# Top-k attention with two feed-forward layers on one core: the first batch's last 64 tokens worked on behind the second batch's first 256, their scores kept in DRAM

## The chip, the cores and the metric

The kernel runs on one core of one Trainium2 chip. The metric is the device time of one execution in microseconds (us). The engines are named as in the profile: PE is the matrix engine (PEld its weight loads), DVE the vector engine, ACT the scalar engine, POOL the general engine, SP the engine that issues nearly all DMAs.

## The reference, cut to what matters

```python
# attention: batch 4, 8 heads, 576 tokens, head dimension 64
scores = (1 / sqrt(64)) * q @ k.T
kth = np.partition(scores, -32, axis=-1)[..., -32]      # 32nd largest of each row
scores = np.where(scores >= kth, scores, -1e9)
attn = softmax(scores) ; x = attn @ v                    # x: 2304 tokens x 512
# two layers, each 512 -> 2048 -> 512, fp32 in and out
h = np.maximum(x @ w_in, 0) ; x = (h * h) @ w_out
h = x @ w_in2 ; out = np.maximum(0.01 * h, h) @ w_out2
```

## The kernel before, in words

**Units, tiles and pairs.** The list `UNITS` cuts the 4 x 576 tokens into nine units (batch, first token, tokens), and its order is the order of the work. Within a unit the kernel takes four head pairs one after the other. A unit of 256 tokens gives four tiles of 128 rows for each head pair, one of 320 tokens gives five, one of 64 tokens gives one (64 rows of each of the two heads). There are 144 tiles in all. Two tiles make a pair; 72 pairs follow each other.

**What is done to a tile.** PE makes its scores (L276, two halves of 288 columns) and ACT copies them to a buffer `s` (L277). DVE finds the 32 largest of each row: four MAX8 (L828) with three MATCH_REPLACE8 (L830) between them. POOL takes a difference of two of the values found (`nb`, L288), ACT turns the scores into weights (L294, L298), and PE transposes them (L312, L325).

**Native and split units.** Units with a number below `NATIVE` multiply weights and values in plain fp32 on PE (L396), and normalise afterwards with a row that PE transposes too (L346). Later units are split: the weights are normalised on POOL (L307), and weights and values are cut into a high and a low part (ACT and DVE for the weights, L317, L318, L334 and L335; ACT and POOL for the values, L113, L115 and L230), so that PE can multiply nine times for each head in the faster fp32r form (L407), with ACT and DVE joining the halves (L412, L413). The buffers of split units exist only when the last native unit is done (`open_late`). Split values are kept in DRAM for the next unit of the same batch (L233, L211).

**Scores kept in DRAM.** Batches 2 and 3 (`EARLY`) have their scores made long before they are used, as filling work in slots 2 to 245. They go through five `stage` buffers to DRAM (L280) and come back 24 slots before their turn (`load_s`, L284). Batches 0 and 1 have their scores made 30 slots ahead, straight into `s`. Keys of a batch are loaded and split once for each head pair (L201, L115, L238), through one raw buffer; the keys of batch 1 take the buffers of batch 0 when the last scores of batch 0 are made.

**Feed-forward blocks.** The tokens, in the order of the units, go into blocks of 512, 256, 384, 512, 256 and 384 tokens (`BLOCKS`). When all tokens of a block are there, its two layers are put into the instruction stream between the attention work: each layer is 16 steps, numbered here 0 to 31 for block 0, 32 to 63 for block 1, 64 to 95 for block 2, 96 to 127 for block 3. A step is 12 matmuls into `h` (L574), an activation on ACT with POOL and in part DVE (L584 to L600), and 8 to 12 matmuls into `acc` (L617 for layer 1, L619 for layer 2). Between the layers ACT and DVE store `xh` and `xl` (L630, L631). During block 0 the weights also come from their raw form: two ACT copies, two DVE operations, one ACT copy and one POOL difference for each of 64 weight tiles (L508, L509, L513, L514, L518, L520).

**What sets the order.** Every piece of attention work has a slot (16 slots to a pair; `z = 16 * p`). The feed-forward work of a block is spread by a rate over the slots until the next block is ready. A scheduler then lays out each engine's fixed instruction order. Tokens of a unit that do not fit into a block are put aside in `spill` (L430) and put into the next one by `unspill` (L447).

Of the kernel before, what the change touches and what calls it, by code (L numbers as in the profile page):

```python
# [24 lines left out]


UNITS = [
    (0, 0, 256), (0, 256, 256), (0, 512, 64), (1, 0, 256), (1, 256, 320),
    (2, 0, 256), (3, 0, 256), (2, 256, 320), (3, 256, 320),
]  # L30

# [6 lines left out]
SPILL = 128  # L38


NATIVE = 3

EARLY = (2, 3)
FILL = (2, 245)
# [12 lines left out]
DLEAD = 30  # L57
LEAD = 24
# [13 lines left out]
def topk_attention_moe_moe2_kernel(  # L72
# [28 lines left out]
    def bank():  # L101
        return psum.tile([P, 512], F, tag="att", name="att", bufs=3)
# [15 lines left out]
    units = []  # L118
# [4 lines left out]
    uhs = []  # L123
    tiles = []
    for u in units:
        for hp in range(NHP):
            n = u["n"]
            uh = dict(u=u, hp=hp, n=n, b=u["b"], first=(u["t0"] == 0), ti=len(tiles), idx=len(uhs),
                      c0=P * (hp % 2) if n == 64 else 0)
            offs = (W - 64 - n, 64)  # L130
            for t in range(2 * n // P):
                lo, hi = t * P, t * P + P
                parts = []
                if lo < n:
                    parts.append((0, offs[0] + lo))
                if hi > n:
                    parts.append((1, offs[1] + lo - n))
                tiles.append(dict(uh=uh, parts=parts, col=uh["c0"] + lo, i=len(tiles)))
            uh["last"] = len(tiles) - 1
            uh["lastA"] = uh["ti"] + (n - 1) // P  # L140
            uhs.append(uh)
    NPAIRS = len(tiles) // 2

    def direct(uh):
        return uh["b"] not in EARLY

    for i, uh in enumerate([uh for uh in uhs if direct(uh)]):
        uh["di"] = i

    def split(uh):  # L150
        return uh["u"]["i"] >= NATIVE

# [5 lines left out]
    for i in range(4):  # L158
        x = const if i < 2 else ahead
# [28 lines left out]
    def at(slot, fn, *a):  # L188
        events.setdefault(slot, []).append((fn, a))


    KT = {}
# [65 lines left out]
    def scores(t, half):  # L258
        uh = t["uh"]
        d = uh["qs"]  # L260
        kt = KT[uh["b"], uh["hp"]]
        if half == 0:
            if direct(uh):
                t["s"] = sbufs[t["i"] % NS]
            else:
                t["s"] = ahead.tile([P, S], F, tag="stage", name="stage", bufs=NST)
        ks = slice(half * HALF, (half + 1) * HALF)
        mm = [(x[:, h, c:c + P], kt[:, h, ks]) for h, c in t["parts"] for x in d]
        if not direct(uh):
            ps = stage_psum.tile([P, 512], F, tag="sp", name="sp", bufs=SPB)  # L270
        elif uh["b"] == 0:
            ps = stage_psum.tile([P, 512], F, tag="sd", name="sd", bufs=SDB)
        else:
            ps = bank()
        for i, (l, r) in enumerate(mm):
            PE.matmul(ps[:, 0:HALF], lhsT=l, rhs=r, start=i == 0, stop=i == len(mm) - 1)  # L276
        ACT.activation(t["s"][:, ks], ps[:, 0:HALF], AF.Copy, scale=0.125)  # L277
        if half == 1 and not direct(uh):
            t["sd"] = dram.tile([P, S], F, tag=f"sd{t['i']}", name=f"sd{t['i']}")
            SP.dma_start(t["sd"], t["s"])  # L280

# [361 lines left out]
    used = {}  # L643
    opened = 16 * (max(uh["last"] for uh in uhs if not split(uh)) // 2) + 35

    def score_slot(ti):
        return 16 * (ti // 2) - DLEAD + 5 * (ti % 2)

    def after(z, *keys):
        return max([z] + [used[k] + 1 for k in keys if k in used])  # L650

    order = []
    for uh in uhs:
        b, hp, i = uh["b"], uh["hp"], uh.get("di")
        z = score_slot(uh["ti"])
        if uh["first"] and direct(uh):
            st = {"i": i}
            st["n"] = len(order)
            order.append(b)
            z0 = after(z - 62, ("kraw", st["n"] - KRB), *[("KT", x, hp) for x in range(b)])  # L660
            at(z0, load_k, b, hp, st)
            for h in range(2):
                at(z0 + 12 * h + 11, split_k, b, hp, st, h)
            used["kraw", st["n"]] = z0 + 23
            assert z0 + 24 <= z
        if (b, hp) not in vdone or split(uh) and VTB < NHP:
            assert not uh["u"]["i"] < NATIVE <= units[max(x["i"] for x in units if x["b"] == b)]["i"]
            vdone.add((b, hp))
            zv = z + DLEAD + 4
            if split(uh):  # L670
                zv = max(zv, opened)
            at(zv, load_v, uh)
            if split(uh):
                at(zv + 6, split_v, uh, 0)
                at(zv + 9, split_v, uh, 1)
        if not direct(uh):
            continue
        uh["qs"] = qsets[i % 2]
        z0 = after(z - 70, ("qraw", i - 2))
        z1 = max(after(z - 20, ("q", i - 2)), z0 + 6)  # L680
        assert z1 + 4 <= z
        at(z0, load_q, uh)
        at(z1, split_q, uh, 0)
        at(z1 + 4, split_q, uh, 1)
        used["qraw", i] = z1 + 4
        used["q", i] = used["KT", b, hp] = score_slot(uh["last"]) + 2

    later_uhs = {}
    for uh in uhs:
# [44 lines left out]
    for p in range(NPAIRS):  # L734
        pr = dict(t=tiles[2 * p:2 * p + 2], p=p)
        pairs.append(pr)
        z = 16 * p
        for i, t in enumerate(pr["t"]):
            if direct(t["uh"]):
                at(z - DLEAD + 5 * i, scores, t, 0)  # L740
                at(z - DLEAD + 2 + 5 * i, scores, t, 1)
            else:
                at(z - LEAD + i, load_s, t)
            if i == 0:
                at(z + 14, shifts, pr)
            at(z + 14 + i, drop, pr, i)
            at(z + 16 + i, expo_sum, pr, i)
            if split(t["uh"]):
                at(z + 20 + i, norm, pr, i)
            at(max(z + 20 + 3 * i, z + 21 + i), pt_main, t)  # L750
        at(z + 18, recip, pr)
        at(z + 26, pt_left, pr)
# [9 lines left out]
    for uh in uhs:  # L762
        if split(uh):
            za, z = 16 * (uh["lastA"] // 2) + 30, 16 * (uh["last"] // 2) + 30
# [7 lines left out]
        for hs in ((0,), (1,)) if apart else ((0, 1),):  # L772
            z = 16 * (uh["lastA"] // 2 if hs == (0,) else uh["last"] // 2) + 30
# [4 lines left out]
        z += nq  # L778
        if uh["u"]["i"] == NATIVE - 1 and uh["hp"] == NHP - 1:
            at(z, open_late)  # L780
# [31 lines left out]
    last = max(events)  # L812
    while slot <= last:
        p, i = divmod(slot, 16)
        if slot >= 0 and p < NPAIRS:
# [7 lines left out]
            x = i % 2  # L823
            t = pr["t"][x]
# [79 lines left out]
```

## Time and profile before

| | |
|---|---|
| median of 3 runs | 1203.64 us (1200.65 to 1205.4) |
| profiled execution | 1204.04 us, of which the trace's span is 1202.3 us |
| busy in the span | PE 1133.4 us (94%), DVE 945.0 (79%), ACT 798.8 (66%), POOL 679.4 (57%) |
| the chain that ended last | PE 56%, DVE 4%, ACT 1%, DMA 1% of the span |
| DMA | 323.25 MB, mean 269 GB/s |

The busy shares are means over stages with different limits. DVE's work ends with the top-k at 957 us; after that it has little to do, while PE has work to the end. So the table says what each engine does, not which one a stage waits for; that is read stage by stage.

### The profile page before, as it was taken

The page shows a single profiled execution, that of the slowest core. Times are in us where ns is not written, and L with a number is a line of the kernel's source. Part 1 is how long each engine was busy: PE and PEld are TensorE (multiplying, and loading weights), DVE is VectorE, ACT ScalarE, POOL GpSimd, SP SyncE. Part 2 cuts the span into 40 slices and gives each one's busy share as a digit, 9 for nine tenths or more (in the row PEclk, how much of TensorE's full clock was granted, in tenths as well). Part 3 has the DMA queues.
Part 4 walks back from the last instruction along what each step waited for, and adds up shares of the span by engine and source line. Part 5 has one row for each costly group of instructions (what it writes and reads, how often), then busy time and mean ns, then how long its engine had stood idle before and what let it go on. Part 6 is the DMA issues. An engine that isn't in the chain of part 4 may idle for free.

```text
span 1202.3 us, 20196 instructions
## 1 busy us (share of the span) xinstructions
PE 1133.4 (94%) x6388; PEld 993.1 (83%) x6388; DVE 945.0 (79%) x1944; ACT 798.8 (66%) x1819; POOL 679.4 (57%) x922
## 2 busy tenths in 40 slices
PE   5999967998899999999999999999999999999998
PEld 4777845886677889988998998888788899999997
DVE  7999999768988899999999999999999920110122
ACT  6999978678999986766665666555675653334322
POOL 7967565677889876456665665545456554004200
PEclk9899978898999999999999999999999999999999
DMA  9868556679889888889988888777676689879974
GB/s 302 288 208 264 204 197 210 219 244 347 312 285 339 297 289 289 291 279 398 332 284 294 266 282 289 221 228 225 198 223 225 191 270 374 253 247 351 353 250 137
DMA packets 110522, 323.25 MB, mean 269 GB/s; under 512 B 17488, under 2 KB 25680, under 8 KB 110416
## 3 DMA queue, kind: packets, MB, share of 16 engines
q1 hardware_dynamic: 107776, 317.24, 78.3%
q10 hardware_dynamic: 2640, 4.72, 1.1%
q8 instruction: 52, 0.85, 0.3%
q14 instruction: 54, 0.44, 0.1%
HBM read 254.54 MB, written 67.37 MB: 268 GB/s over the span
## 4 chain that ended last, share of the span: by engine, by line
PE 56%; DVE 4%; ACT 1%; DMA 1%; issue 0%; POOL 0%; SPq 0%; ACTq 0%
PE h L574 24%; PE acc L617 12%; PE acc L619 12%; PE att L407 3%; PE att L312 3%; DVE m L828 2%; DVE w L830 1%; PE att L325 1%; DVE PTs L318 1%; DMA vraw<-in_v_dram 0%; PE att L276 0%; DVE xl L631 0%; ACT y L634 0%; DMA wi<-wd 0%; ACT e L298 0%
## 5 line engine op out<-in xcount | busy, mean ns | idle before, releaser
L574 PE MATMUL h<-xh,wi 128*128 128x512 f32 (+2 forms) x1280 | 349.2, 345 | 14.4 <-ACT gb L596 4.9
L828 DVE MAX8 m<-w 128x8 f32<-128x576 f32 x432 | 312.9, 747 | 1.4
L574 PEld LDWEIGHTS h<-xh,wi 128*128 128x128 f32 x1280 | 227.5, 191 | 41.7 <-ACT gb L596 6.6
L830 DVE MATCH_REPLACE8 w<-m,w 128x576 f32<-128x576 f32 x288 | 213.2, 742 | 0.7
L574 PE MATMUL h<-xl,wi 128*128 128x512 f32 (+2 forms) x640 | 207.3, 342 | 2.3 <-DVE xl L631 1.3
L600 POOL TENSOR_TENSOR gl<-ga,gh 128x512 fp32r<-128x512 f32 (+2 forms) x160 | 163.3, 1021 | 44.6 <-ACT gh L599 40.6
L617 PE MATMUL acc<-gh,wo 128*128 128x512 f32 (+2 forms) x768 | 155.9, 341 | 0.0
L619 PE MATMUL acc<-wo,gh 128*128 128x512 f32 x576 | 152.4, 399 | 1.5 <-ACT gh L599 1.5
L597 POOL TENSOR_TENSOR ga<-ga,gb 128x512 f32<-128x512 f32 (+2 forms) x80 | 81.6, 1020 | 107.9 <-ACT gb L596 106.9
L294 ACT ACTIVATE e<-s,m 128x576 f32<-128x576 f32 x144 | 112.5, 782 | 39.2 <-DVE m L828 32.1
L617 PEld LDWEIGHTS acc<-gh,wo 128*128 128x128 f32 x768 | 126.2, 189 | 10.9 <-ACT gh L585 0.4
L574 PEld LDWEIGHTS h<-xl,wi 128*128 128x128 f32 x640 | 121.2, 191 | 14.8 <-DVE xl L631 3.7
L619 PEld LDWEIGHTS acc<-wo,gh 128*128 128x128 f32 x576 | 103.8, 188 | 21.6 <-ACT gh L599 2.6
L586 POOL TENSOR_TENSOR ga<-ga 128x512 f32<-128x512 f32 (+2 forms) x80 | 66.4, 830 | 84.7 <-ACT gh L585 76.5
L298 ACT ACTIVATE e<-e,nb 128x576 f32<-128x576 f32 x144 | 110.8, 774 | 4.7 <-POOL nb L288 4.4
L828 DVE MAX8 m<-s 128x8 f32<-128x576 f32 x144 | 103.8, 747 | 8.3 <-ACT s L277 5.1
L830 DVE MATCH_REPLACE8 w<-m,s 128x576 f32<-128x576 f32 x144 | 106.9, 743 | 0.4
L312 PE MATMUL att<-ident,e 128*128 128x128 f32 x576 | 88.5, 281 | 18.3 <-ACT e L298 13.9
L584 ACT ACTIVATE ga<-h 128x512 f32<-128x512 f32 (+2 forms) x80 | 39.2, 490 | 85.5 <-PE h L574 77.1
L307 POOL TENSOR_SCALAR e<-e,rc 128x576 f32<-128x576 f32 x108 | 80.0, 753 | 28.2 <-DVE rc L303 26.2
L312 PEld LDWEIGHTS att<-ident,e 128*128 128x128 f32 x576 | 70.2, 144 | 29.9 <-ACT e L298 18.2
L599 ACT ACTIVATE gh<-ga 128x384 fp32r<-128x384 f32 (+2 forms) x112 | 58.4, 522 | 44.7 <-POOL ga L597 34.8
(94 smaller groups left out, 2153.0 us busy)
## 6 DMA issues: line engine op xcount, KB each, us to landing
wi<-wd SPq DMA_DIRECT2D x160, 512.0 KB, 5.0
wo<-wd SPq DMA_DIRECT2D x160, 512.0 KB, 5.1
wraw<-in_w_dram SPq DMA_DIRECT2D x64, 512.0 KB, 5.8
sd<-stage SPq DMA_DIRECT2D x72, 288.0 KB, 3.5
s<-sd SPq DMA_DIRECT2D x72, 288.0 KB, 4.5
wd<-wi SPq DMA_DIRECT2D x32, 512.0 KB, 5.3
wd<-wo SPq DMA_DIRECT2D x32, 512.0 KB, 6.2
kraw<-in_k_dram SPq DMA_DIRECT2D x16, 576.0 KB, 4.5
```

The lines of the kernel that those rows point to most:

```text
L294: ACT.activation(t["e"], t["s"], AF.Prelu, bias=pr["m8"][:, i, 31:32], scale=-1.0, alpha=1.0 / FAR)
L298: ACT.activation(e, e, AF.Exp, bias=pr["nb"][:, i:i + 1], scale=-FAR, accum_out=pr["sum"][:, i:i + 1])
L307: POOL.tensor_scalar(e, e, pr["rc"][:, i:i + 1], 1.0, op0=OP.mult, op1=OP.mult)
L312: PE.transpose(ps[:, j * P:(j + 1) * P], t["e"][:, j * P:(j + 1) * P], ident)
L574: PE.matmul(h[:, 0:n], lhsT=wi[:, w, c * P:(c + 1) * P], rhs=x[c][y][:, 0:n], start=cnt == 0, stop=cnt == 3 * NK - 1)
L586: POOL.tensor_tensor(a[:, 0:n], a[:, 0:n], a[:, 0:n], op=OP.mult)
L597: POOL.tensor_tensor(a[:, 0:n], a[:, 0:n], b[:, 0:n], op=OP.subtract)
L600: (DVE if j >= GLD else POOL).tensor_tensor(gl[:, 0:n], a[:, 0:n], gh.bitcast(F)[:, 0:n], op=OP.subtract)
L617: PE.matmul(acc[c][:, 0:n], lhsT=wo[:, w, cs], rhs=g[:, 0:n], start=first, stop=last)
L619: PE.matmul(acc[c], lhsT=g[:, cs], rhs=wo[:, w, :], start=first, stop=last)
L828: cur["dve"] = DVE.max(out=m8[:, x, 8 * r:8 * r + 8], in_=t["s"] if r == 0 else t["w"])
L830: cur["dve"] = DVE.match_replace(out=t["w"], in_to_replace=m8[:, x, 8 * r:8 * r + 8], in_values=t["s"] if r == 0 else t["w"], imm_value=NEG)
```

## The change

Three things change together. The unit (batch 0, tokens 512 to 575) moves behind the unit (batch 1, tokens 0 to 255). It is no longer native but split (`NATIVE` is 2). Its scores are still made while batch 0's keys are there, right behind those of the unit before it, but now go to DRAM and come back 24 slots before their turn (`KEPT`).

```diff
 UNITS = [
-    (0, 0, 256), (0, 256, 256), (0, 512, 64), (1, 0, 256), (1, 256, 320),
+    (0, 0, 256), (0, 256, 256), (1, 0, 256), (0, 512, 64), (1, 256, 320),
...
-NATIVE = 3
+NATIVE = 2
+
+KEPT = 3
...
+    def kept(uh):
+        return uh["u"]["i"] == KEPT
+
+    def score_slot(ti):
+        return 16 * (ti // 2) - DLEAD + 5 * (ti % 2)
+
+    for uh in uhs:
+        uh["zs"] = score_slot(uh["ti"])
+        if kept(uh):
+            ahead_of = [x for x in uhs if x["b"] == uh["b"] and x["hp"] == uh["hp"] and x["i0"] < uh["i0"]][-1]
+            uh["zs"] = score_slot(ahead_of["last"]) + 5
+    in_time = sorted([uh for uh in uhs if direct(uh)], key=lambda uh: uh["zs"])
...
-            if direct(uh):
+            if direct(uh) and not kept(uh):
                 t["s"] = sbufs[t["i"] % NS]
             else:
                 t["s"] = ahead.tile([P, S], F, tag="stage", name="stage", bufs=NST)
...
-        if half == 1 and not direct(uh):
+        if half == 1 and (kept(uh) or not direct(uh)):
             t["sd"] = dram.tile([P, S], F, tag=f"sd{t['i']}", name=f"sd{t['i']}")
             SP.dma_start(t["sd"], t["s"])
...
-        used["q", i] = used["KT", b, hp] = score_slot(uh["last"]) + 2
+        used["q", i] = used["KT", b, hp] = (z if kept(uh) else score_slot(uh["last"])) + 2
...
-            if direct(t["uh"]):
+            if kept(t["uh"]):
+                at(t["uh"]["zs"], scores, t, 0)
+                at(t["uh"]["zs"] + 2, scores, t, 1)
+            if kept(t["uh"]) or not direct(t["uh"]):
+                at(z - LEAD + i, load_s, t)
+            else:
                 at(z - DLEAD + 5 * i, scores, t, 0)
                 at(z - DLEAD + 2 + 5 * i, scores, t, 1)
-            else:
-                at(z - LEAD + i, load_s, t)
```

Block 1 (256 tokens) is now exactly the unit (batch 1, 0 to 255), so nothing is spilled into block 2; block 0 has eight pairs of attention work beside it until block 1 is complete, where it had ten, and block 1 has twelve, where it had ten.

Line numbers below are each kernel's own: L115 is L117 after the change, L238 is L252, L288 is L302, L407 is L421, L520 is L534, L574 is L588, L617 is L631.

On POOL, where block 0 begins, before (`KT` and `kraw` are keys, `wi` and `wo` weights, `xl_650` the low part of block 0's input):

```order
L115 TENSOR_SCALAR KT<-kraw 128x576 x2
L238 TENSOR_TENSOR KT<-kraw,KT 64x576
L520 TENSOR_TENSOR wi<-wc,wi 128x512
L238 TENSOR_TENSOR KT<-kraw,KT 64x576
L520 TENSOR_TENSOR wo<-wc,wo 128x512
L288 TENSOR_TENSOR nb<-m_2297 128x2
L302 TENSOR_SCALAR sum<-sum 128x2
```

The same place after the change:

```order
L445 TENSOR_TENSOR xl_650<-xn,xh_649 128x256
L269 TENSOR_TENSOR q_78<-qraw,q_77 128x256
L534 TENSOR_TENSOR wi<-wc,wi 128x512
L534 TENSOR_TENSOR wo<-wc,wo 128x512
L302 TENSOR_TENSOR nb<-m_2373 128x2
L316 TENSOR_SCALAR sum<-sum 128x2
```

The key split of the fourth head pair no longer stands between the first weight differences and ahead of `nb`; it stands further up, ahead of other `nb` rows.

On PE, in step 3 of block 0, before (`PT` and `VN` are the native weights and values):

```order
L574 MATMUL h<-xh_649,wi 128x512 x4
L346 MATMUL att<-ident,rc 128x128 x2
L617 MATMUL acc<-gh,wo 128x512 x8
L396 MATMUL att<-PT,VN 128x64 x20
L617 MATMUL acc<-gl,wo 128x512 x4
```

The unit's 72 split matmuls after the change, in steps 33 and 34 of block 1 (36 of them; the other 36 stand in steps 37 and 38):

```order
L588 MATMUL h<-xh_3272,wi 128x256
L588 MATMUL h<-xl_3273,wi 128x256
L588 MATMUL h<-xh_3272,wi 128x256 x4
L421 MATMUL att<-PTs,VT 128x64 x17
L633 MATMUL acc<-wo,gl 128x512 x4
...
L588 MATMUL h<-xh_3272,wi 128x256 x4
L421 MATMUL att<-PTs,VT 128x64 x19
L631 MATMUL acc<-gh,wo 128x256 x8
```

Forty native matmuls (20 in step 3, 20 in step 7) are gone from block 0, and 72 split ones have come into block 1. On DVE the order moves as a whole: ahead of the last weight conversion of block 0 stand the first MAX8 of 56 tiles before and of 53 after; ahead of block 1's `xl` rows (its middle) 71 and 65; ahead of block 2's 96 and 92; ahead of block 3's 128 and 128.

## Rows read from the trace of the kernel before

**Rows 1.** Stretches of the span: busy us of each engine, clock, DMA.

```profile
core 0: us, PE busy (x) PEld busy (x) DVE busy (x) ACT busy (x) POOL busy (x), PEclk, DMA share, GB/s
...
200.00:329.00 129.00, 120.64 (x572) 98.58 (x573) 105.58 (x205) 106.32 (x223) 96.11 (x103) 0.94 0.80 276
329.00:426.00 97.00, 93.11 (x450) 76.20 (x450) 85.25 (x158) 91.83 (x188) 82.73 (x81) 0.99 0.88 302
426.00:510.00 84.00, 83.21 (x631) 79.17 (x629) 82.34 (x172) 62.05 (x151) 50.42 (x84) 1.00 0.87 294
510.00:658.00 148.00, 143.65 (x914) 136.31 (x913) 146.25 (x308) 93.04 (x216) 92.66 (x140) 1.00 0.92 319
658.00:745.00 87.00, 84.80 (x472) 76.34 (x471) 86.22 (x184) 56.32 (x125) 53.65 (x73) 0.98 0.84 274
```

**Rows 2.** Timeline of ACT and PE where block 3 begins.

```profile
744.78 0.42 ACT L428 ACTIVATE xh<-xf 128x256 fp32r<-128x256 f32 x1 [0.52 <-DVE w L830]
...
745.25 0.50 PE L574 MATMUL h<-xh,wi 128*128 128x512 f32 x1 [0.21 <-ACT xh L428]
```

**Rows 3.** Timeline of DVE: start us, us, what, count.

```profile
505.73 0.74 DVE L830 MATCH_REPLACE8 w<-m,s 128x576 f32<-128x576 f32 x1
...
509.50 1.07 DVE L631 TENSOR_TENSOR xl<-acc,xh 128x256 fp32r<-128x256 f32 x3
...
705.12 1.40 DVE L828 MAX8 m<-s 128x8 f32<-128x576 f32 x2
```

**Rows 4.** Timeline of POOL, ACT and PE where block 0 begins.

```profile
175.30 1.31 POOL L115 TENSOR_SCALAR KT<-kraw 128x576 fp32r<-128x576 f32 x2 [3.14 <-DMA kraw<-in_k_dram]
...
179.51 1.41 POOL L238 TENSOR_TENSOR KT<-kraw,KT 64x576 fp32r<-64x576 f32 x1
...
182.22 0.20 POOL L288 TENSOR_TENSOR nb<-m 128x2 f32<-128x2 f32 x1
...
182.86 0.76 ACT L298 ACTIVATE e<-e,nb 128x576 f32<-128x576 f32 x1
...
183.76 0.48 PE L312 MATMUL att<-ident,e 128*128 128x128 f32 x1 [9.18 <-ACT e L298]
```

**Rows 5.** Timeline of PE: the native 64-token matmuls and what follows them.

```profile
217.28 6.40 PE L396 MATMUL att<-PT,VN 128*128 128x64 f32 x40
...
225.48 0.63 PE L574 MATMUL h<-xh,wi 128*128 128x512 f32 x1
225.91 0.63 PE L574 MATMUL h<-xl,wi 128*128 128x512 f32 x1
...
250.09 1.00 PE L396 MATMUL att<-PT,VN 128*128 128x64 f32 x8
...
251.23 4.34 PE L396 MATMUL att<-PT,VN 64*128 64x64 f32 x32
```

**Rows 6.** Short stretches, columns as in rows 1.

```profile
221.00:228.00 7.00, 7.00 (x23) 5.84 (x23) 5.82 (x14) 2.90 (x7) 3.39 (x6) 0.51 0.80 273
...
281.00:288.00 7.00, 6.66 (x21) 5.49 (x22) 4.73 (x10) 4.75 (x10) 6.71 (x8) 0.65 1.01 359
```

**Rows 7.** Groups by form: line, engine, what, count, busy us, mean ns.

```profile
L294 ACT ACTIVATE e<-s,m 128x576 f32<-128x576 f32 x144 | 112.5, 782 | 39.2 <-DVE m L828 32.1 <-PE att L325 6.6 <-issue 0.3
...
L318 DVE TENSOR_TENSOR PTs<-att,PTs 128x512 fp32r<-128x512 f32 x108 | 72.9, 678 | 3.8 <-ACT PTs L317 2.9
...
L413 DVE TENSOR_TENSOR xf<-att,tmp 64x256 f32<-64x256 f32 x24 | 10.0, 416 | 0.7 <-ACT tmp L412 0.3
```

**Rows 8.** Timeline of PE in block 1.

```profile
472.74 0.28 PE L574 MATMUL h<-xh,wi 128*128 128x256 f32 x1
472.86 0.28 PE L574 MATMUL h<-xl,wi 128*128 128x256 f32 x1
```

**Rows 9.** Waits of DVE, 140 to 460 us: total, times, longest us.

```profile
DVE wc L513 <- ACT att L509: 24.8, 19, 4.5
```

**Rows 10.** DMA issues of the page: count, KB, us to landing.

```profile
s<-sd SPq DMA_DIRECT2D x72, 288.0 KB, 4.5
```

More of the change, by code (lines that the diff above doesn't have):

```diff
@@ L127, in topk_attention_moe_moe2_kernel @@
             n = u["n"]
-            uh = dict(u=u, hp=hp, n=n, b=u["b"], first=(u["t0"] == 0), ti=len(tiles), idx=len(uhs),
+            uh = dict(u=u, hp=hp, n=n, b=u["b"], first=(u["t0"] == 0), i0=u["i"], ti=len(tiles), idx=len(uhs),
                       c0=P * (hp % 2) if n == 64 else 0)
@@ L145, in direct @@
         return uh["b"] not in EARLY
-    for i, uh in enumerate([uh for uh in uhs if direct(uh)]):
+    def kept(uh):
[8 more added lines that the diff above has]
+    in_time = sorted([uh for uh in uhs if direct(uh)], key=lambda uh: uh["zs"])
+    for i, uh in enumerate(in_time):
         uh["di"] = i
@@ L644, in topk_attention_moe_moe2_kernel @@
     opened = 16 * (max(uh["last"] for uh in uhs if not split(uh)) // 2) + 35
-    def score_slot(ti):
-        return 16 * (ti // 2) - DLEAD + 5 * (ti % 2)
     def after(z, *keys):
@@ L652, in topk_attention_moe_moe2_kernel @@
     order = []
-    for uh in uhs:
+    for uh in in_time + [uh for uh in uhs if not direct(uh)]:
         b, hp, i = uh["b"], uh["hp"], uh.get("di")
-        z = score_slot(uh["ti"])
+        z = uh["zs"]
         if uh["first"] and direct(uh):
@@ L666, in topk_attention_moe_moe2_kernel @@
         if (b, hp) not in vdone or split(uh) and VTB < NHP:
-            assert not uh["u"]["i"] < NATIVE <= units[max(x["i"] for x in units if x["b"] == b)]["i"]
             vdone.add((b, hp))
-            zv = z + DLEAD + 4
+            zv = score_slot(uh["ti"]) + DLEAD + 4
             if split(uh):
```

## The prediction

> **What bounds the kernel now.** I read the stretches first, then the timelines where one gives way to the next. Block 0 runs from 200 to 426 us, and there DVE is busy 105.6 of 129 us and 85.3 of 97: it idles 35 us in 226 [rows 1]. PE (120.6 of 129) bounds the first part and ACT (91.8 of 97) the second, because the weights are converted there too; one wait of DVE is named, 24.8 us for ACT's copies of raw weights [rows 9]. From 426 us to 745 us DVE is the full engine: 82.3 of 84, 146.3 of 148, 86.2 of 87 us, and PE stands at 83.2, 143.7 and 84.8 beside it [rows 1]. So block 0 costs DVE idle time, and blocks 1 and 2 are paid for in DVE work, with PE just behind. Block 3 then starts when its last tokens are there: ACT stores the last `xh` at 744.78 us, and the first matmul of block 3 waits 0.21 us for it at 745.25 [rows 2]. From there to the span's end at 1202.3 are 457 us, and PE has work in nearly all of it. The end is therefore set by when DVE has done the tiles of block 3 (the last of them, tile 104, gets its first MAX8 at 705.8, the second of the two that start at 705.12 [rows 3]), plus a tail that the change leaves alone. The work of DVE up to there is nearly the same before and after, so the question is how much DVE idles on the way.
>
> **Block 0's start.** At 175.30 POOL waits 3.14 us for keys, then spends 1.31, 1.40 (a second row of its form, at 176.69) and 1.41 us on their split, and `nb` stands behind that, at 182.22; ACT's exponentials wait for `nb` (182.86) and PE's transposes for them, 9.18 us idle [rows 4]. The order after the change has these keys further up, since the keys of batch 0 are free earlier. 3.14 + 1.31 + 1.40 + 1.41 is 7.3 us; I take 7 off the start of block 0, at least 0 (if `nb` waits for the two weight differences instead), at most 7.3. DVE is busy through most of that stall, so it gains some 2 us itself.
>
> **Native matmuls out of block 0.** The trace has two records for each fp32 matmul. The first group takes 6.40 us, the second 1.00 and 4.34 us [rows 5]: 11.7 us. Behind the first group the granted clock is 0.51 from 221 to 228 us [rows 6], and a matmul of 512 columns starts every 0.43 us (225.48 and 225.91) [rows 5]. About 4.4 us of feed-forward matmuls, to 228.0, run at 1.2 GHz, and would take half: 2.2 us more. Against it, 9 more split matmuls of 256 columns fall into these 16 steps, 9 x 0.12 [rows 8] = 1.1 us. PE bounds there, so 11.7 + 2.2 - 1.1 = 12.8; I take 12, since step and conversion chain do not shrink for sure. Bounds: 6 and 13.
>
> **Two pairs fewer beside block 0.** The order has 22 tiles transposed in the 32 steps before, 20 after, and 26 fewer score matmuls (13 fewer ACT copies). On ACT two tiles are four passes of about 0.78 us [rows 7] with copies besides; I put it at 6 us of ACT time in the part that ACT bounds, between 0 and 9. So block 0's end comes 7 + 12 + 6 = 25 us earlier, between 8 and 29.
>
> **What DVE loses.** The order puts the last weight conversion behind 53 tiles instead of 56. A tile is four MAX8 of 0.70 us (1.40 for two) and three MATCH_REPLACE8 of 0.74 us [rows 3], which overlap a little: about 4.8 us. Three tiles and their small work are some 17 us, so in block 0 DVE idles about 25 - 17 = 8 us less. The gap closes in the first half of block 1: its middle stands behind 65 tiles instead of 71, so 3 more tiles are missing, but PE's 16 steps are not shorter. PE is full there (83.2 of 84), loses some 18 matmuls of 288 columns, 12 transposes and 27 split matmuls of other units, and gets 72 of 64 columns. The trace has no fp32r matmul of 64 columns. One of 256 starts every 0.12 us [rows 8]; in proportion to columns it would be 0.03. So 72 cost 2.2 to 8.6 us; I take 6.5, nearer to the upper end, since all their weights have to be loaded, and PE comes out even within 3 us. DVE then idles some 9 us more in this half. Block 1's `xl`, at 509.50 [rows 3], comes at 509.5 - 25 = 484.5; DVE's work to there is smaller by about 27, so its idle time grows by 2.
>
> The Trainium skill, "TensorE: Matmul & The Clock Gate", section "LDWEIGHTS (loading the stationary operand)", says that the load takes the number of columns divided by 1.2 GHz, whatever the rows: 107 ns for 128 columns. By that estimate the 72 would be 7.7 us and the sum 1 us later; the 0.12 us of the trace at 256 columns neither contradict nor prove it.
>
> **What follows.** From block 1's middle to tile 104 stand 39 tiles instead of 33. Six tiles of 4.8 us are 29 us of a full DVE. Tile 104 then comes at 705.8 - 25 + 29, about 4 us later; its range by the bounds is 8 earlier to 21 later. Extra DVE work for the split unit is in these figures: four operations of 0.68 us, eight joins below the 0.42 us of 256 columns [rows 7], about 4 us. PE, which was full, gets gaps in blocks 1 and 2, and both blocks start when their tokens are there, not later. The spill that falls away (eight small copies and as many differences) lay beside other work. Scores go to DRAM in slots 124 to 222 and come back 24 slots, some 17 us at 16 slots for a pair of about 11.5 us, before their turn, where a load takes 4.5 us [rows 10]: nothing. Four more loads and stores of values in block 1 are hidden the same way, unless the two buffers for split values hold one back; then PE's row of 64-column matmuls waits, and DVE's full work covers some of it. **Sum:** 1204.04 (profiled; 0.4 above the median) + 4 = **1208 us**.
>
> **Rivals.**
> - *Block 0 does not give the time back: slower.* Place: the conversion chain of block 0, where DVE waits 24.8 us on ACT's copies [rows 9] and DMA stands at 0.80 and 0.88 [rows 1]. If a step is held by that chain, removing PE and ACT work shortens it by 8 to 16 us and not 25, while the six tiles still come later: 1204 + 29 - 16 = 1217, at worst 1225. It decides from the point where block 0 gains less than 23 us.
> - *Block 1's first half shortens with DVE: faster.* If PE has slack there that its busy share hides, the 9 us of new idle time do not arise: 1208 - 9 = 1199; with 4 us more from block 0, 1195. For it: matmul ends are modelled. Against it: DVE and PE are both full in this stretch.
> - *PE's clock.* After the gap ahead of 281 us the granted clock was 0.65 over 7 us [rows 6], 2.4 us lost. In blocks 1 and 2 PE would be idle some 40 us of 270. If that came in gaps like this one, ten of them would lose 24 us of PE time, which the 40 us still hold, so the end moves little unless they fall ahead of block 3: 1208 to 1214. The Trainium skill, the same page, section "HAM oscillation — how this bites in real kernels", says that waits between bursts of matmuls drop the clock again and again, which speaks against a change that starves PE. The trace agrees where gaps are long (9.18 us [rows 4]).
> - *It does not do what it says.* The kept scores could come late and hold DVE. At 17 us ahead for 4.5 that would need a queue four times as slow: 1210.
>
> **How the numbers follow.** 0.5% of 1204 is 6 us, about what a measurement of this kernel tells from no change; so faster is below 1198, slower above 1210. Forecast (1200 to 1210, its own range): 0.45. First rival 0.25; second 0.2; clock 0.07; late scores 0.03. The forecast's upper end and these give: faster 0.2, same 0.43, slower 0.37. The range takes in the second rival's 1195 and reaches to 1221, two thirds up the first rival.
>
> **What would show it.** Right: the transposes at the start of block 0 follow each other without the 9 us gap; no half clock at 221 us; block 1's `xl` at 480 to 490; DVE above 97% from there to tile 104, and that at 705 to 715; PE with gaps ahead of block 2 and block 3; block 3's start waiting for `xh`. Wrong: block 1's `xl` after 492 (first rival), DVE idle under 5 us in block 1's first half (second rival), or DVE waiting for `s` from DRAM.

## The result and the profile after

The changed kernel takes **1211.6 us** (median of 5 runs, 1210.3 to 1213.64) against 1203.64 (1200.65 to 1205.4): ratio 1.0058, 95% interval 1.0038 to 1.0078. It is slower, by just over half a per cent; 1208 was forecast, with 1195 to 1221 as the range. The profiled execution took 1213.64 us with a span of 1211.9, 9.6 us more than the span of before. That is 2 us above the median, so the working below accounts for 9.6 us of one execution, of which the medians confirm 8.

The stretches that answer to [rows 1]: from, to, length, then busy us (count) of PE, PEld, DVE, ACT, POOL, the granted clock, the DMA share and GB/s.

```profile
200.00:329.00 129.00, 121.64 (x567) 98.59 (x566) 114.80 (x216) 118.88 (x236) 114.38 (x116) 0.99 0.93 331
329.00:426.00 97.00, 93.31 (x492) 78.26 (x491) 77.61 (x149) 84.35 (x176) 80.30 (x83) 1.00 0.87 313
426.00:510.00 84.00, 82.30 (x642) 79.18 (x641) 74.59 (x160) 57.05 (x148) 45.39 (x77) 1.00 0.84 298
510.00:658.00 148.00, 139.75 (x863) 132.32 (x862) 146.50 (x311) 91.95 (x210) 89.04 (x135) 0.98 0.85 297
658.00:745.00 87.00, 79.22 (x434) 70.28 (x433) 86.15 (x182) 54.54 (x120) 49.08 (x68) 0.93 0.80 267
```

DVE is fuller in the first row (114.80 of 129, where it was 105.6) and emptier in the next two (77.61 and 74.59, where it was 85.3 and 82.3). PE, nearly full in the last two rows before, idles 8 us in each now. The last raw weight is converted at 394.2 us and not at 426, block 1's first step begins at 411.70 and not at 434.81, and block 1's `xl` stands here (DVE's timeline: start, us, what, count), with tile 104, the second of two, behind it:

```profile
486.55 1.41 DVE L645 TENSOR_TENSOR xl<-acc,xh 128x256 fp32r<-128x256 f32 x4
...
711.81 1.41 DVE L841 MAX8 m<-s 128x8 f32<-128x576 f32 x2
```

The row of four `xl` in the change has to be set against the first `xl` of before, which stands one row ahead of the three of [rows 3]:

```profile
508.51 0.41 DVE L631 TENSOR_TENSOR xl<-acc,xh 128x256 fp32r<-128x256 f32 x1
```

So a lead of 22.0 us at `xl` (486.55 against 508.51) has become a delay of 6.7 us at tile 104 (712.5 against 705.8). PE's timeline ahead of block 3, which answers to [rows 2] (in brackets the idle time before, and what ended it):

```profile
732.65 0.55 PE L421 MATMUL att<-PTs,VT 128*128 128x256 f32 x1 [1.77 <-DVE PTs L332]
733.82 2.07 PE L421 MATMUL att<-PTs,VT 128*128 128x256 f32 x8 [0.61 <-DVE PTs L332]
738.80 1.97 PE L326 MATMUL att<-ident,e 128*128 128x128 f32 x8 [2.91 <-POOL e L321]
...
750.53 2.50 PE L588 MATMUL h<-xh,wi 128*128 128x512 f32 x5 [4.89 <-ACT xh L442]
752.83 1.91 PE L588 MATMUL h<-xl,wi 128*128 128x512 f32 x4
754.53 1.83 PE L326 MATMUL att<-ident,e 128*128 128x128 f32 x8
756.20 0.38 PE L339 MATMUL att<-ident,e 128*64 128x128 f32 x2
...
757.13 0.40 PE L588 MATMUL h<-xl,wi 128*128 128x512 f32 x1
757.37 0.39 PE L588 MATMUL h<-xh,wi 128*128 128x512 f32 x1
```

PE has no step of block 2 left and waits for one tile after the other: POOL's normalised weights, DVE's low parts, at last 4.89 us for ACT's `xh` (0.21 before). Block 3 starts 5.3 us later (750.53 against 745.25; by its start is meant the matmul that waits for the last `xh`, three matmuls of its first step having run ahead of it in both kernels), and at half clock: its matmuls start every 0.46 us (five of them from 750.53 to 752.83), where they start every 0.24 from 757.13 on. The granted clock over two short stretches:

```profile
732.00:756.00 24.00, 13.12 (x44) 10.53 (x45) 23.82 (x51) 10.13 (x22) 4.36 (x10) 0.51 0.37 126
757.00:770.00 13.00, 13.00 (x63) 10.60 (x62) 12.90 (x28) 7.91 (x17) 7.88 (x10) 1.00 0.67 210
```

From 750.53 to 756.34 PE does work that takes half as long at 2.4 GHz: 2.8 us lost. From block 3's start to the end are 461.4 us, where it was 457.0.

DVE has also more to do. Of before and of after, the groups that differ (line, what, count, busy us, mean ns, idle before):

```profile
L335 DVE TENSOR_TENSOR PTs<-att,PTs 64x128 fp32r<-64x128 f32 x12 | 3.4, 284 | 1.5 <-ACT PTs L334 1.1
L427 DVE TENSOR_TENSOR xn<-att,rb 128x64 f32<-128x64 f32 x4 | 0.9, 216 | 1.2 <-PE att L396 1.2
```

```profile
L332 DVE TENSOR_TENSOR PTs<-att,PTs 128x512 fp32r<-128x512 f32 x112 | 75.2, 678 | 11.3 <-ACT PTs L331 10.4
L349 DVE TENSOR_TENSOR PTs<-att,PTs 64x128 fp32r<-64x128 f32 x16 | 4.5, 284 | 0.8 <-ACT PTs L348 0.3
L427 DVE TENSOR_TENSOR xf<-att,tmp 64x64 f32<-64x64 f32 x8 | 1.7, 217 | 6.5 <-PE acc L631 3.2 <-POOL xl L445 3.2
```

Four evictions of 0.678 (112 for the 108 of [rows 7]) and four of 0.284, eight joins of 0.217, less four `xn` of 0.216: 4.7 us; DVE's busy time on the page grew by 4.0 (949.0 against 945.0).

### The profile page after: what moved, and what is told of

Its sections match the earlier page's. It is cut to its first block, busy times and chain, and to the rows that moved or that the text cites. A ratio compares the mean times of both kernels' runs of the same rounds, so it can differ in the third digit from the quotient of the medians.

```text
span 1211.9 us, 20264 instructions
## 1 busy us (share of the span) xinstructions
PE 1136.3 (94%) x6376; PEld 995.0 (82%) x6376; DVE 949.0 (78%) x1956; ACT 802.7 (66%) x1823; POOL 686.6 (57%) x926
## 4 chain that ended last, share of the span: by engine, by line
PE 67%; DVE 12%; ACT 12%; DMA 4%; issue 3%; POOL 2%; ACTq 0%; SPq 0%; POOLq 0%; DVEq 0%
PE h L588 27%; PE acc L633 14%; PE acc L631 13%; DVE m L841 5%; PE att L421 4%; DVE w L843 4%; PE att L326 3%; PE att L410 2%; ACT e L312 2%; ACT stage L291 2%; ACT e L308 2%; PE sp L290 1%; PE att L290 1%; ACT s L291 1%; DMA vraw<-in_v_dram 1%
## 5 line engine op out<-in xcount | busy, mean ns | idle before, releaser
L588 PE MATMUL h<-xh,wi 128*128 128x512 f32 (+2 forms) x1280 | 351.6, 346 | 13.5 <-ACT xh L442 6.8
L588 PEld LDWEIGHTS h<-xh,wi 128*128 128x128 f32 x1280 | 227.6, 191 | 40.5 <-ACT xh L442 7.8
L588 PE MATMUL h<-xl,wi 128*128 128x512 f32 (+2 forms) x640 | 207.1, 342 | 0.9 <-DVE xl L645 0.6
L631 PE MATMUL acc<-gh,wo 128*128 128x512 f32 (+2 forms) x768 | 154.9, 341 | 3.0 <-ACT gh L599 3.0
L631 PEld LDWEIGHTS acc<-gh,wo 128*128 128x128 f32 x768 | 125.8, 188 | 14.8 <-ACT gh L599 3.3
L588 PEld LDWEIGHTS h<-xl,wi 128*128 128x128 f32 x640 | 121.1, 191 | 13.9 <-DVE xl L645 2.6
L421 PE MATMUL att<-PTs,VT 128*128 128x256 f32 (+2 forms) x504 | 87.4, 302 | 9.6 <-DVE PTs L332 4.4
L321 POOL TENSOR_SCALAR e<-e,rc 128x576 f32<-128x576 f32 x112 | 82.7, 752 | 24.1 <-DVE rc L317 21.5
L421 PEld LDWEIGHTS att<-PTs,VT 128*128 128x128 f32 x504 | 74.8, 194 | 16.0 <-ACT PTs L348 3.6
```

What stands on the lines that cost most here:

```text
L321: POOL.tensor_scalar(e, e, pr["rc"][:, i:i + 1], 1.0, op0=OP.mult, op1=OP.mult)
L421: PE.matmul(ps, lhsT=l, rhs=r, start=i == 0, stop=i == len(mm) - 1)
L588: PE.matmul(h[:, 0:n], lhsT=wi[:, w, c * P:(c + 1) * P], rhs=x[c][y][:, 0:n], start=cnt == 0, stop=cnt == 3 * NK - 1)
L631: PE.matmul(acc[c][:, 0:n], lhsT=wo[:, w, cs], rhs=g[:, 0:n], start=first, stop=last)
```

## The experiments

**Theory A**: up to block 3's start DVE sets the time, so the end moves with DVE's idle time beside block 0 and in block 1's first half, and with what DVE has to do in addition. The rivals stand with each run. All were timed against the kernel before on the same chip; "the change" is 1.0058 in this measure. A number that sums them up, chosen behind the runs, is DVE's idle time up to 510 us, 510 less its busy time there, as in this row of the change (columns as above; DVE 456.95, so 53.0 idle):

```profile
0.00:510.00 510.00, 463.54 (x2580) 390.74 (x2581) 456.95 (x929) 433.35 (x1020) 379.00 (x500) 0.97 0.84 291
```

**1. The unit split, but left third, scores direct.** Half of the change: split form without the move.

```diff
-    (0, 0, 256), (0, 256, 256), (1, 0, 256), (0, 512, 64), (1, 256, 320),
+    (0, 0, 256), (0, 256, 256), (0, 512, 64), (1, 0, 256), (1, 256, 320),
-KEPT = 3
+KEPT = 99
```

> The unit of 64 tokens is split as in the change, but keeps its old place (third), its scores are made directly and block 1 is 64 + 192 tokens again. Theory A (the change loses because DVE idles beside block 0 and the first half of block 1, where fewer tiles are left to do, and is the full engine after that): the 12 us of native matmuls go from block 0, and the order has 56 and 71 tiles ahead of the two marks as before, so DVE's idle time falls by up to 12 us against 4 us of new DVE work: 1196 us, between 1192 and 1200. Theory B (the split unit itself is what costs: 72 matmuls, joins and value loads in a full PE): 1205 to 1212.

Measured: 1215.9 us, ratio 1.0083 [1.0058, 1.0108]. Theory A's range was missed, and the upper end of theory B's (1212) was passed too. The last conversion comes at 427.9 us, so taking the native matmuls out does not shorten block 0 (426 before). Block 3 starts at 749.47, 4.2 us later than before, with the same idle time up to 510 (48.8 against 48.9) and the same 4 to 5 us of added DVE work: the split form costs DVE that much, and it arrives at block 3's start in full. Behind it this kernel loses another 8.7 us (465.7 from there to the end against 457.0). Most of that is in the trace: PE waits 2.87 us for block 3's first activation (0.69 before), and two thirds of the first 10.5 us run at 1.2 GHz; another stretch at that clock follows at 872 us. The table on PE behind block 3's start, below, has the sums.

**2. Keys of batch 1 later.**

```diff
-            z0 = after(z - 62, ("kraw", ...
+            z0 = after(z - (24 if b == 1 else 62), ("kraw", ...
```

> The change, with the keys of batch 1 loaded and split 24 slots ahead of the first scores instead of 62, so that their POOL work falls beside the start of block 0 again. Theory A with its term for the keys: the 7 us stall at block 0's start comes back and the end moves 3 to 7 us later, to 1214 to 1219. Rival (the stall was hidden behind the weight conversions and POOL's place in it was chance): same as the change within 2 us, 1210 to 1213.

Measured: 1211.82 us, 1.0042 [1.0026, 1.0058]. The run tells nothing of the keys: the last of their splits still runs at 150 to 156 us, as in the change, because the other bounds in that line decide the slot. It stands as a repeat of the change in nearly the same order, and shows that 1.0042 and 1.0058 are the same.

**3. The kept unit's joins off DVE.**

```diff
-        DVE.tensor_tensor(uh["xf"][mine, 0:n], ps[mine], uh["tmp"][mine, 0:n], op=OP.add)
+        if kept(uh):
+            ACT.activation(uh["xf"][mine, 0:n], ps[mine], AF.Copy)
+            POOL.tensor_tensor(uh["xf"][mine, 0:n], uh["xf"][mine, 0:n], uh["tmp"][mine, 0:n], op=OP.add)
+        else:
+            DVE.tensor_tensor(...)
```

> The change, with the eight small joins of the 64-token unit made by ACT (both halves) and POOL (the sum) instead of ACT and DVE. In the trace of the change DVE stands still for 7.8 of the us from 420 to 430, in order, for these joins and for scores behind them. Theory A as predicted (PE is full in the first half of block 1, so DVE idles there whatever it waits for): DVE waits for scores instead, 1208 to 1212. Rival (the joins in DVE's fixed order hold up the top-k): 5 to 8 us earlier, 1203 to 1207.

Measured: 1220.76 us, 1.0119 [1.0093, 1.0145]: slower than either side expected. DVE's waits between 200 and 510 us in this kernel (us in total, times, longest):

```profile
DVE m L845 <- ACT s L291: 18.7, 8, 8.5
```

In the change the same wait was 9.6 us, and the joins waited 6.4 us (3.2 for PE's `acc`, 3.2 for POOL's `xl`). So the 6.4 us left and 9.1 us came back one place further on, at the scores: the MAX8 behind them starts at 429.54 where the change has 429.75, so the joins were not what held DVE there. Block 3 starts at 750.36, as in the change; from there to the end it takes 5.3 us longer than the change (466.7).

**4. Block 0's steps spread over 160 slots, as they were before.** In the change they have 128. Block 1's steps get 160 for 192, and block 2's tokens a buffer of their own, so that the two can overlap.

```diff
-SETS = (0, 1, 0, 1, 0, 2)
+SETS = (0, 1, 2, 1, 0, 2)
+MORE = 32
...
+        more = {0: MORE, 1: -MORE}.get(j, 0)
-... / max(nxt - rslot[j] - 1, 40))
+... / max(nxt - rslot[j] - 1 + more, 40))
...
```

> The change, with the feed-forward steps of block 0 spread over 160 slots (ten pairs) as before instead of 128, and block 1 over the following 160; block 2's input gets buffers of its own so that block 0 may last longer. The order has 56 tiles ahead of block 0's last weight conversion (53 in the change, 56 before) and 68 ahead of block 1's middle (65, 71). Theory A: half or more of the loss of DVE time is undone while the native matmuls and the key stall stay gone: 1198 to 1205. Rival (where the tiles stand beside the blocks does not matter, the split unit's work or the gap ahead of block 3 does): 1209 to 1214.

Measured: 1203.86 us, 0.9983 [0.9967, 0.9998]: 8 us better than the change, and a hair better than before. DVE idles 42.3 us up to 510, 10.8 less, and the last `xh` ahead of block 3 comes at 738.70, so that block 3 starts at 739.17, 11.4 us earlier. The last raw weight is converted at 415.8 us here, 21.6 later than in the change.

**5, 6, 7. The same with 0, 48 and 24 slots.** `MORE` is the only edit to version 4; with 0 only the buffers' change is left.

> Control for the spread version: block 0's steps over 128 slots and block 1's over 192, as in the change, only block 2's tokens in buffers of their own. Theory A (DVE's idle time beside block 0 and block 1's first half sets the end, so the spread did it): like the change, 1211 us (1208 to 1214). Rival (the freed token buffers did it): like the spread version, 1202 to 1206, and block 2 would start earlier.

> Spread version with 48 slots moved instead of 32: block 0 over 176 slots, block 1 over 144. Theory A: a little more of block 0 is filled, but it was nearly even at 32, so the rest is small: 1200 to 1205. Rival (block 1 has too few slots left, PE becomes the full engine and holds DVE there): 1206 to 1212.

> Spread version with 24 slots moved. 0 slots gave 1212, 32 gave 1204, 48 gave 1212. If the gain grows evenly with the slots up to 32 (DVE's idle time beside block 0 filled bit by bit): 1205 to 1207. Rival (32 hit an order that happens to fit, so what counts is which step meets which tile): 1209 to 1213.

Measured: 1212.07 (1.0057 [1.0044, 1.0071]), 1212.12 (1.0062 [1.0047, 1.0078]) and 1217.95 (1.0092 [1.0074, 1.0110]). The buffers do nothing, so the spread made the gain; but it does not grow with the slots. At 24 DVE idles 58.0 us up to 510, at 48 it is 49.0. With 24 slots DVE waits 13.2 us for ACT's `s` and 12.6 us ahead of the joins between 200 and 510 us, where with 32 it is 4.9 and 8.0. With 48 slots 4.1 us less idle time than in the change moves block 3's start by only 0.2, since 3.5 us more of DVE's work stands ahead of it (698.6 us busy up to there, 695.1 in the change). This points to which step meets which tile in the fixed order; no run takes that apart. At 24 slots the end lies above both expectations.

**8. Ten us of DVE work less between 530 and 645 us.** The fourth search of 20 tiles reads only 72 of the 576 values of a row; the rest is left out.

```diff
+SHORT = range(72, 92)
+                wide = S // 8 if r == 3 and t["i"] in SHORT else S
-                ... in_=t["s"] if r == 0 else t["w"])
+                ... in_=t["s"] if r == 0 else t["w"][:, 0:wide])
```

> The change, with the fourth MAX8 of tiles 72 to 91 over the first 72 of 576 values only (the rest of the row is left out of that search). 20 x about 0.6 us = 12 us of DVE work less between about 530 and 645 us. Theory A (DVE is the full engine there and sets block 3's start): block 3's first full step at 738 to 743 instead of 750.5, end at 1200 to 1204. Rival (PE's total work sets the end): 1210 to 1213, with 12 us more idle time of DVE ahead of block 3.

Measured: 1206.74 us, 1.0011 [0.9999, 1.0023]. The short searches take 0.222 us for 0.747 (20 x 0.525 = 10.5 us), and DVE happened to idle 2.8 us less before. Block 3's start comes 13.75 us earlier, at 736.78, so up to there DVE sets the time, us for us. The end moves by 5.7 us only (0.47%). PE's timeline there:

```profile
736.78 0.80 PE L590 MATMUL h<-xh,wi 128*128 128x512 f32 x1 [2.92 <-ACT xh L444]
...
745.53 0.80 PE L590 MATMUL h<-xh,wi 128*128 128x512 f32 x1 [3.25 <-ACT ga L600]
746.12 0.63 PE L590 MATMUL h<-xl,wi 128*128 128x512 f32 x1
```

Block 3 waits again, 3.25 us for the first activation, and runs at half clock (0.43 us a matmul). Part of DVE's lead is lost again there: a stretch of 15.2 us, in which PE idles 3.26 us and the granted clock is 0.63, where the same place in run 1 has 2.87 us and 0.67:

```profile
749.47:760.00 10.53, 7.66 (x25) 5.90 (x24) 10.44 (x22) 5.41 (x11) 2.69 (x5) 0.67 0.52 186
736.78:752.00 15.22, 11.96 (x35) 9.40 (x36) 15.13 (x33) 6.32 (x13) 5.51 (x8) 0.63 0.24 76
```

(first run 1, then this one). Theory A holds up to block 3's start, its range for the end doesn't.

**9, 10. Matmuls that nobody reads, in the gaps ahead of block 3.** Five of 512 columns ahead of each group of transposes and products of the last head pair, and ten behind the last; in the second version only the ten.

```diff
+    def keep_on(uh, ps, n):
+        if uh["hp"] == NHP - 1 and uh["u"]["i"] == gate:
+            for _ in range(n):
+                PE.matmul(ps[:, 0:4 * P], lhsT=vt[:, 0, 0, :], rhs=..., start=True, stop=True)
+        keep_on(t["uh"], ps, KEEP_ON[0])          # in pt_main, and in av_split
+        if h == 1:
+            keep_on(uh, bank(), KEEP_ON[1])
```

> The change, with 40 matmuls of 512 columns whose result nobody reads in PE's gaps ahead of block 3 (9.4 us at full clock, of 12.4 us idle there). If the half clock behind the gaps costs what the matmuls from 750.5 to 756.3 show, 2.9 us: 1207 to 1210, granted clock 1.0 from 750 on. Rival (DVE, busy over 98% up to 965 us, sets the end and hides it): 1210.5 to 1213.

> The change with only the last 10 of the matmuls that nobody reads, behind the last product of weights and values ahead of block 3, where nothing that block 3 waits for stands behind them but one product and two transposes. If the half clock behind the gap is worth 2.9 us and can be had without delaying the tokens: block 3's first full step at 750 to 751, full clock from there on, 1207 to 1210. Rival (the clock does not rise in so short a stretch, or DVE hides it): 1210.5 to 1213.

Measured: 1210.8 (1.0049 [1.0035, 1.0063]) and 1212.05 (1.0043 [1.0027, 1.0059]). The first has the clock at full speed from 750 on:

```profile
750.00:757.00 7.00, 5.68 (x29) 4.12 (x28) 6.84 (x15) 4.20 (x9) 1.22 (x2) 1.00 0.49 163
```

But block 3's start is at 752.77, 2.2 us later, since the fillers from 743 to 749 us ran at half clock themselves and stood ahead of the last products. In the second the fillers run from 745.99 on, the clock is up at 750 and falls again behind a gap of 1.64 us (0.67 from 740 to 760), and the start is at 753.67. Both lie among the repeats of the change (1.0042 to 1.0058). So these runs alone do not show that the half clock costs the end anything. In the first the stretch from block 3's start to block 4's is 2.8 us shorter than in the change (217.3 against 220.1), just what the change loses at half clock there, but the start itself is 2.2 later.

**11, 12. PE's steps of block 2 held to the order of the tiles**, 16 slots longer, so that they fill the gaps ahead of block 3: on the change, and on version 4.

```diff
+DELAY = {3: 16}                               # {1: 32, 3: 16} on version 4
+            cur["pe"] = PE.transpose(...)     # in pt_main
+                    with behind("pe") if (j, layer) in groups[2] and cnt == 0 else ExitStack():
                         PE.matmul(h[:, 0:n], ...
...
```

> The change, with each step of block 2 queued on PE behind the transposes of the tiles that stand before it, and block 2's steps spread over 16 slots more, so that the last of them stand in the gaps ahead of block 3. Theory G (PE's idle time ahead of block 3, 12.4 us from 705 to 785, and the half clock behind it, about 3 us, are lost for good, since PE is full from there to the end): idle time there 2 to 5 us, 1199 to 1204. Rival D (DVE, busy over 98% to 970 us, sets the end): 1210 to 1213. Rival C (PE, held to the tiles' order, idles as much earlier in block 2): 1208 to 1213, with gaps before 705.

> Both together: the spread version (32 slots) and block 2's steps held to the tiles' order with 16 slots more. Theory G: the spread version still idles 11.5 us from 705 to 785, so 8 to 12 us less than its 1203.9: 1192 to 1197, which beats both kernels. Rivals D and C: 1202 to 1206.

Measured: 1220.97 (1.0138 [1.0117, 1.0159]) and 1204.28 (0.9994 [0.9980, 1.0008]). Theory G fell. The two stretches, first of the change, then of run 11:

```profile
545.00:705.00 160.00, 151.74 (x894) 143.00 (x893) 158.54 (x334) 97.38 (x212) 98.57 (x142) 0.98 0.84 288
705.00:785.00 80.00, 67.58 (x327) 56.60 (x326) 79.32 (x168) 45.79 (x97) 36.77 (x52) 0.85 0.65 212
```

```profile
545.00:705.00 160.00, 141.94 (x801) 129.94 (x799) 156.92 (x332) 92.95 (x199) 88.58 (x133) 0.94 0.77 257
705.00:785.00 80.00, 74.82 (x399) 64.49 (x399) 79.28 (x169) 51.00 (x108) 45.16 (x60) 1.00 0.78 263
```

PE's idle time ahead of block 3 went from 12.4 to 5.2 us, and that of 545 to 705 rose from 8.3 to 18.1. On version 4 it went from 11.5 to 0.4 and from 1.6 to 14.0, with the same end. In these two runs PE's gaps were put elsewhere, not filled, as theory A says of time by which DVE is behind.

**All runs together** (worked out from the rows; DVE's idle time up to 510 us, block 3's start, the span, and the span less the idle time):

| kernel | idle | block 3 | span | difference |
|---|---|---|---|---|
| 32 slots (4) | 42.3 | 739.2 | 1199.1 | 1156.8 |
| 32 slots, held (12) | 44.1 | | 1202.9 | 1158.8 |
| 48 slots (6) | 49.0 | 750.3 | 1210.3 | 1161.3 |
| 0 slots (5) | 51.6 | 749.1 | 1210.3 | 1158.7 |
| keys (2) | 51.8 | 749.3 | 1209.3 | 1157.5 |
| fillers (9) | 52.2 | 752.8 | 1209.0 | 1156.8 |
| the change | 53.0 | 750.5 | 1211.9 | 1158.9 |
| last fillers (10) | 53.7 | 753.7 | 1211.8 | 1158.1 |
| joins (3) | 54.8 | 750.4 | 1217.1 | 1162.3 |
| 24 slots (7) | 58.0 | 754.6 | 1215.0 | 1157.0 |
| split in place (1) | 48.8 | 749.5 | 1215.2 | 1166.4 |
| held (11) | 54.8 | | 1221.8 | 1167.0 |
| before | 48.9 | 745.3 | 1202.3 | 1153.4 |

In the first ten rows the span goes with the idle time over 16 us, within 3 us of 1159.5. The kernel before lies some 5 us below them, and has 4.0 us of DVE work less. Runs 1 and 11 don't fit, by some 7 us, and were set apart after the fact. (Run 8 has other work and isn't listed. Each span is that of one execution, up to 2.8 us off the median of its kernel.)

**PE behind block 3's start**, to the same place in block 4's first step: the length, PE's idle time, half of the time that PE was busy at 1.2 GHz (which is what it lost there), and the rest, in us (worked out from the traces; the ends of matmuls are modelled, so tenths are rough).

| kernel | length | idle | lost at half clock | rest |
|---|---|---|---|---|
| before | 218.2 | 2.8 | 0 | 215.4 |
| the change | 220.1 | 1.1 | 2.8 | 216.1 |
| 32 slots (4) | 220.6 | 3.4 | 1.9 | 215.3 |
| fillers (9) | 217.3 | 2.0 | 0 | 215.3 |
| split in place (1) | 226.8 | 5.4 | 4.8 | 216.6 |
| joins (3) | 228.3 | 5.6 | 5.7 | 217.0 |
| short searches (8) | 229.1 | 5.6 | 6.9 | 216.6 |

The rest is 215 to 217 us while the length varies by 12; in the other seven kernels it is 213.1 to 217.9. So in this stretch what PE idles or loses at half clock arrives at its end in full, and that is why the tails of runs 1, 3 and 8 are long. From there to the end all take 238 to 242 us. (DVE's last MAX8 ends at 963.3 us before and not at 957, and at 972.4 in the change, so DVE's top-k ends about where block 4 starts.)

## Why the prediction came out as it did

**Up to block 3's start the mechanism was the one forecast**, and the 5.3 us there are of the forecast's size (4). They are DVE's time, up to 745.25 before and up to 750.53 in the change:

```profile
0.00:745.25 745.25, 684.96 (x3898) 595.33 (x3898) 693.86 (x1426) 579.72 (x1353) 511.76 (x701) 0.97 0.83 280
0.00:750.53 750.53, 683.14 (x3876) 593.69 (x3876) 695.07 (x1429) 583.03 (x1356) 517.51 (x703) 0.96 0.83 288
```

DVE's idle time grew by 4.1 us (51.4 to 55.5) and its work ahead of the start by 1.2. The 4 to 5 us of the split unit are all ahead of it, but five searches and replacements of the top-k fewer stand there (two MAX8, three MATCH_REPLACE8). Both are forecast terms (9 us of new idle time in block 1's first half, less what block 0 gains; 4 us for the split unit), and experiments 1, 4 and 8 show by moving them that DVE's time arrives at block 3's start: +4.2 for 4 to 5 us of work, -11.4 for 10.8 of idle time, -13.75 for 13.3 of both. PE's gaps ahead of blocks 2 and 3, and the start waiting for `xh`, came too. The other 4.3 us are the tail, which the forecast took as unchanged. So the end lies above the forecast's own 1200 to 1210, where the rival on PE's clock had its range (1208 to 1214, with a chance of 0.07), and the condition that this rival named, gaps ahead of block 3, was met.

**Block 0's start, 7 us:** mis-sized. The keys did move and POOL's 3.14 us wait is gone, but PE's transposes start only 3.9 us earlier, at 179.88 (183.76 in [rows 4]), still after a gap, now of 3.10 us:

```profile
179.88 1.97 PE L326 MATMUL att<-ident,e 128*128 128x128 f32 x8 [3.10 <-ACT e L312]
```

The first full step is 2.7 us earlier, and by the eighth conversion the lead is 0.6 us (206.4 against 207.0). No run isolates the keys.

**Native matmuls, 12 us, and two pairs fewer, 6 us:** together too small, and split between them wrong. From the eighth conversion to the last the change takes 187.8 us for 219.0, 31 us less; no half clock follows at 221 (1.00 over the 7 us that show 0.51 in [rows 6]). But split in place (1) the last conversion is at 427.9, so removing the native matmuls alone shortens nothing there: what shortens block 0 is the move, by 33.7 us (427.9 to 394.2). With 160 slots in place of 128 (4) 21.6 of them are gone again, so most of it is that block 0's steps are spread over fewer slots. The conversions ended 7 us earlier than the 401 forecast, PE's steps did not: block 1's first comes 23.1 us earlier, where 25 was forecast. Of these 23.1 the lead at the start is 0.6 and not 7, and the rest 22.5 and not 18, so that the sum came out nearly right is luck. The range given with it was not their sum either: their bounds add up to 6 and 29, not 8 and 29.

**Block 1's first half:** the price of the 64-column matmuls was 6.5, with 2.2 to 8.6 as bounds. PE's timeline:

```profile
417.00 1.98 PE L421 MATMUL att<-PTs,VT 128*128 128x64 f32 x17
418.81 1.17 PE L633 MATMUL acc<-wo,gl 128*128 128x512 f32 x4
...
421.24 2.21 PE L421 MATMUL att<-PTs,VT 128*128 128x64 f32 x19
423.28 1.20 PE L631 MATMUL acc<-gh,wo 128*128 128x256 f32 x8
```

1.81 us for 17 and 2.04 for 19 are 0.107 each, 7.7 for 72; from block 1's first step to its first `xl` it takes 74.9 us (411.70 to 486.55) for 73.7 (434.81 to 508.51), so the missing 1.2 us is about what the half grew by; no run isolates it. The Trainium skill, "TensorE: Matmul & The Clock Gate", section "LDWEIGHTS (loading the stationary operand)", puts the time of a load at its columns divided by 1.2 GHz, by estimate 107 ns for 128 columns: the spacing of these matmuls agrees, while the record of one load lasts 194 ns in the mean:

```profile
L421 PEld LDWEIGHTS att<-PTs,VT 128*128 128x128 f32 x504 | 74.8, 194 | 16.0 <-ACT PTs L348 3.6 <-DVE PTs L349 3.2 <-DVE PTs L332 2.7
```

DVE in this half, from block 1's first step to its first `xl`, first before, then in the change:

```profile
434.81:508.51 73.70, 73.04 (x577) 70.86 (x576) 72.65 (x154) 54.28 (x134) 40.55 (x72) 1.00 0.86 290
411.70:486.55 74.85, 74.24 (x604) 72.77 (x602) 60.89 (x131) 51.03 (x134) 40.78 (x68) 1.00 0.88 314
```

It idles 14.0 us where it was 1.1: 12.9 more, for 9 forecast. Ahead of block 1's first step it idles 9.0 less (8 forecast), so up to `xl` 4 more (2 forecast). It waits for PE's `acc`, POOL's `xl` and ACT's `s`, in this order on its timeline:

```profile
424.47 0.23 DVE L427 TENSOR_TENSOR xf<-att,tmp 64x64 f32<-64x64 f32 x1 [3.22 <-PE acc L631]
426.50 0.48 DVE L427 TENSOR_TENSOR xf<-att,tmp 64x64 f32<-64x64 f32 x2 [1.80 <-POOL xl L445]
429.75 0.76 DVE L841 MAX8 m<-s 128x8 f32<-128x576 f32 x1 [2.77 <-ACT s L291]
```

**Block 1's `xl`** came at 486.55 (484.5 forecast; 480 to 490). The forecast took 25 us off 509.50, which is the second `xl`; off the first, at 508.51, it would have been 483.5, so the lead is 3 us short of it. **Tile 104**, 29 us of DVE work later by forecast, came at 712.5 (705 to 715): 225.9 us behind the first `xl`, where it was 197.3, so 28.7 more. DVE is 99% busy from 510 to 658 and from 658 to 745.

**The tail, "unchanged":** this is the term that was mis-sized most, 4.3 us of the 5.6 by which the span's growth of 9.6 exceeds the 4 forecast; the other 1.3 are block 3's start. The rival on PE's clock had named the place (gaps ahead of block 3, half clock behind them). It had put PE's idle time in blocks 1 and 2 at some 40 us; it is 22.6 from block 1's first step to block 3's start (7.6 before), and the clock alone costs the 2.8 us. Of the 4.3, 1.9 stand ahead of block 4 (2.8 more lost at half clock, 1.7 less idle, 0.7 of the rest) and 2.4 behind it, of which 1.03 us is a wait for a weight tile's DMA at 1007.53 and the remainder is open. The profiled execution is also the longest of the five. Removing the half clock (9) did not bring the end back beyond the measurement, since the fillers delayed block 3's start. Behind that start the kernels above take from 456 us (9) to 468 us (8), and the table on PE says where: in idle time and half clock, much of it at a wait of 2.87 to 3.25 us for block 3's first activation, which the change does not have. Why that wait comes was not followed up. The Trainium skill, the same page, section "HAM oscillation — how this bites in real kernels", warns of such waits between bursts of matmuls; the trace agrees, with half clock from 732.26 to 756.15 us, among gaps of 0.61 to 4.89 us.

The other rivals did not come. Block 0 gave back its time (23 to 32 us, no 8 to 16); block 1's first half did not shorten with DVE; no wait of DVE for `s` from DRAM is in the trace.

## What to carry to other kernels

Where two engines are nearly full, moving a unit of work out of one stage into the next need not save it, and here it did not: count the idle time of the fuller engine up to the point where the next stage waits for it, and add the work that the new form costs that engine. PE's gaps in such a stretch were the other engine's time here, and putting PE's work into them moved them in both runs. Behind that point PE is the full engine, and there its idle time and its time at half clock are to be counted in turn. After a change of order, try the pace of the neighbouring stages again (here 32 slots gave back 8 us), and expect an uneven answer: 24 and 48 slots gave nothing or less.

## What the runs showed of the hardware that was not expected

- A split matmul of 64 columns costs 0.107 us from start to start, not much less than one of 256 columns (0.12 [rows 8]); each has weights of its own to load.
- During the first 20 native matmuls of 64 columns (40 records, 217.28 to 223.7 us) the clock fell, to 0.51 from 221 to 228 with PE busy all the time [rows 6]; without them it stays at 1.00 there, in the change and in run 1. During the second 20, from 250.09 on, it did not fall. In the change it falls at 732.26, in a gap of 1.77 us, and stays down over gaps of up to 4.89 us until 756.15. In run 9, with matmuls in the first gaps, it falls only at 742.4, and those in the later gaps ran at half clock.
- The spread over 24, 32 and 48 slots gave 1.0092, 0.9983 and 1.0062: in this kernel, with its fixed order on each engine, a change of pace by 8 slots was worth 13 us.
